# The softmax sums of twelve batches: three accumulating transfers over tap planes instead of VectorE reductions

## The chip, the cores and the metric

One Trainium2 chip, of which the kernel uses one core. A core has five engines that run side by side, each taking its own instructions strictly in order: TensorE (PE, matrix products into PSUM), VectorE (DVE, elementwise work and reductions), ScalarE (ACT, functions such as exponential and ReLU, and copies out of PSUM), GpSimd (POOL) and SyncE (SP). POOL and SP mainly issue transfers (DMAs), which the core's 16 DMA engines carry out. An engine that meets an instruction whose input is not there yet waits, and everything behind that instruction on the same engine waits with it. The metric is device time in microseconds (us) of one execution; the median of several runs is given.

## What is computed

A dynamic convolution followed by a layer with two hidden products. For each of 8 sequences of 4160 positions and 8 heads, a softmax over 7 taps gives weights, with which the last 7 positions of `x` are summed; each head owns 24 of 192 channels. The result, 33280 rows of 192, goes through two products with 1024 hidden columns, of which the larger is kept, and through a product back to 192 columns.

```python
w = np.exp(weight_gen - max over taps)
w = w / (np.sum(w, axis=-1, keepdims=True) + 1e-09)
out[b, s, h, :] = sum over k of w[b, s, h, k] * x_pad[b, s + k, h, :]      # h: 24 channels
g = np.maximum(out @ w1, out @ w2)                                         # 192 -> 1024
return g @ w_out                                                           # 1024 -> 192
```

The kernel takes no maximum off. It forms the weight as exp(w - ln(sum of exp(w))), so that a softmax costs one exponential, a sum over 7 taps, a logarithm, a subtraction and a second exponential.

## The kernel before

**Tiling.** The 33280 rows lie as 128 partitions x 260 columns, a column being one row for each partition. Columns go in 17 batches (`BATCHES`): 0 to 15 of 16 columns, and one last of 4. A batch of index 2 to 15 is worked in two units of 8 columns, batches 0 and 1 in four units of 4. TensorE's work is counted in 260 tiles: a unit of 8 columns has 8 tiles, each one chunk of 128 hidden columns for all 8 columns of the unit. Tiles go in groups, two at a time for the first 16, three at a time later (`GROUPS`).

**One batch's way through the engines.**

1. `load_wg` (L104): weights of a batch, 128 x 896 (16 columns x 8 heads x 7 taps) from HBM into `wg_t`, issued on POOL.
2. `exp_sum` (L135, ScalarE): exponential of `wg_t` into `e_t`. The taps of one column and head lie side by side, 7 elements.
3. `red` (L147, VectorE): the sum of 7 neighbours, 128 x 448 to 128 x 64, twice per batch, into `sum_t`.
4. `ln` (L151, ScalarE): logarithm of the 128 x 128 sums in place.
5. `shift` (L156, VectorE): subtracts it from `wg_t`, in three parts.
6. `weights` (L167, ScalarE): second exponential, into `en_t` in bf16, each weight twice, read from `wg_t` with a step of 7 elements.
7. `mul` (L182, VectorE): 7 taps x 8 columns of `x` times the weights into `m_t`, 128 x 10752 in bf16; then `adds` (L198, L204, L207, VectorE): the 7 taps are summed pairwise into `y_t`.
8. `transpose` (L216, SP): `y_t` is transposed by a transfer into `yt`. On POOL, `gate` (L224), a copy of one column of `yt`, holds the loads behind it until that transpose has landed: for a unit at column 0, `xb_t` for 8 columns (L114) and `wg_t` of three batches later (L104); for a unit at column 8, `xb_t` for the next batch and its halo, a copy of 6 columns within SBUF (`load_halo`, L127).
9. `hid_tile` (L299, TensorE) makes the hidden products from `yt`, `relu` (L309, ScalarE) takes them out of PSUM into `rd_t`, `out_first` and `out_second` (L351, L339, TensorE) make the output products, `evac` (L395, ScalarE) copies them to `o_t`, and SP stores them (L407).

**What sets the order.** The order of every engine is the order in which the program is written. TensorE's groups are the frame. ScalarE's softmax steps for batches from 3 on stand in a table, `due`, by the index of a tile, and are written out with the group that holds that tile (`softmax_steps`). A long step (exponentials) is put off by a group where a long one has just stood in a group with few outputs. The rows for batch c:

```python
ln_at = -2 if c == 4 else 0 if c < 8 else 2 if c < 11 else 4
parts_.append((16 * (c - 2) + ln_at, False, lambda c=c: ln(c)))
parts_.append((16 * (c - 3) + (4 if c < 8 else 7), True, lambda c=c: exp_sum(c)))
```

VectorE's steps stand in `extra(t)`, which is called for each tile. The two halves of `red` are written beside the adds of an earlier batch, and the three parts of `shift` beside others:

```python
adds(c, 0, beside=lambda i, of: shift(c + 1, i, of) if c + 1 < NB else None)
...
adds(b + 1, 8, beside=lambda i, of: red(b + 3, i, 2) if b + 3 < NB and i < 2 else None)
```

`e_t` has two buffers, `sum_t` three, `wg_t` four and `yt` six.

Of the kernel before, what the change touches and what calls it, by code (L numbers as in the profile page):

```python
# [9 lines left out]
FP32 = mybir.dt.float32  # L10
BF16 = mybir.dt.bfloat16
I32 = mybir.dt.int32
AF = mybir.ActivationFunctionType
ALU = mybir.AluOpType
# [3 lines left out]
def _sub(base: bass.AP, off: int, dims):  # L18
    ap = [list(base.ap[0])] + [[int(s), int(c)] for s, c in dims]
    return dataclasses.replace(base, offset=base.offset + off, ap=ap)  # L20
# [3 lines left out]
def kernel(  # L24
# [9 lines left out]
    nc = tc.nc  # L34

    B, S, D = x.shape
    H, K = weight_gen.shape[2], weight_gen.shape[3]
    F = moe_w1.shape[1]
    P = 128
# [10 lines left out]
    BATCHES = [(c, min(16, CPP - c)) for c in range(0, CPP, 16)]  # L50
    NB = len(BATCHES)


    def pieces(b):
        n = BATCHES[b][1]
        at, done = [], 0
        for w in (4, 4, 4, 4) if b < 2 else (8, 8) if n == 16 else (n,):
            at.append((done, w))
            done += w
        return at  # L60
# [18 lines left out]
    psm = ctx.enter_context(tc.tile_pool(name="psm", bufs=3))  # L79
# [17 lines left out]
    wg_ts, xb_ts, e_ts, s_ts, en_ts, y_ts, yt_ts = {}, {}, {}, {}, {}, {}, {}  # L97
# [33 lines left out]
    def exp_sum(b, i=0, of=1):  # L131
        if i == 0:
            e_ts[b] = pe_.tile([P, BATCHES[b][1] * WGC], FP32, name="e_t", tag="e")
        w = BATCHES[b][1] * WGC // of
        nc.scalar.activation(out=e_ts[b][:, i * w:(i + 1) * w], in_=wg_ts[b][:, i * w:(i + 1) * w], func=AF.Exp)  # L135

    def part(b, i, of):

        n = BATCHES[b][1]
        h0, h1 = n * i // of * H, n * (i + 1) // of * H  # L140
        return slice(h0, h1), h0 * K, [[K, h1 - h0], [1, K]]

    def red(b, i=0, of=1):
        if i == 0:
            s_ts[b] = psm.tile([P, BATCHES[b][1] * H], FP32, name="sum_t", tag="sum")
        hs, at, ap = part(b, i, of)
        nc.vector.reduce_sum(out=s_ts[b][:, hs], in_=_sub(e_ts[b], at, ap), axis=AX.X)  # L147

    def ln(b, i=0, of=1):
        s_t = s_ts[b][:, part(b, i, of)[0]]  # L150
        nc.scalar.activation(out=s_t, in_=s_t, func=AF.Ln)  # L151

# [6 lines left out]
    def weights(b, o):  # L159

        w = dict(pieces(b))[o]
        if b not in en_ts:
            en_ts[b] = pen.tile([P, 16 * WGC * 2], BF16, name="en_t", tag="en")
        J = 2 if w == 4 and b < 2 else 1
        N = w * H // J
        for j in range(J):
            nc.scalar.activation(  # L167
                out=_sub(en_ts[b], (o * WGC + j * N * K) * 2, [[2 * N, K], [2, N], [1, 2]]),
                in_=_sub(wg_ts[b], (o * H + j * N) * K, [[1, K], [K, N], [0, 2]]), func=AF.Exp,
            )  # L170
# [62 lines left out]
    def half(j):  # L233
        return slice(64 * j, 64 * j + 64)
# [191 lines left out]
    OUTS, c = [[], [], []], 0  # L426
# [85 lines left out]
    with tc.tile_pool(name="pstage", bufs=1) as pstage:  # L512
# [7 lines left out]
        for p0, p1 in ((1, 16), (16, P)):  # L520
            nc.sync.dma_start(  # L521
                out=xs[p0:p1, 0:PAD * D],
                in_=bass.AP(tensor=x.tensor, offset=(p0 * CPP - PAD) * D,
                            ap=[[CPP * D, p1 - p0], [1, PAD * D]]),
# [20 lines left out]
        for wi, wsrc in enumerate((moe_w1, moe_w2)):  # L545
            for h in range(2):
                nc.sync.dma_start(
                    out=ws["T", wi][half(h), :],
                    in_=bass.AP(tensor=wsrc.tensor, offset=P * F + h * HF, ap=[[F, 64], [1, HF]]),
# [11 lines left out]
        for step in (exp_sum, red, ln, shift):  # L561
            for i in range(2):
                step(0, i, 2)
# [6 lines left out]
        for o in (0, 4, 8, 12):  # L570
            weights(0, o)
        nc.vector.tensor_copy(out=xb_ts[0][:, PAD * D:(PAD + 4) * D],
                              in_=xs[:, PAD * D:(PAD + 4) * D])
# [36 lines left out]
        def keep_warm(times):  # L610
# [11 lines left out]
            out=wo[:, :].rearrange("p (f d) -> p f d", d=D),  # L622
            in_=bass.AP(tensor=moe_w_out.tensor, offset=0, ap=[[D, P], [P * D, FCH], [1, D]]),
# [11 lines left out]
        hid_tile(0)  # L635
        relu(rd, 0, 1)
        exp_sum(1)
        hid_tile(1)
        relu(rd, 1, 1)
        w_diff(1, nc.vector.tensor_copy)  # L640
        sum_transpose(1)
        red(1)
        mul(0, 8)
        hidden(1)
        ln(1)
        shift(1)
        mul(0, 12)
# [39 lines left out]
        mul(1, 4)  # L687
        relu(rd, 7, 1)
        exp_sum(2)
        red(2)  # L690
        adds(1, 4, True)
        sum_transpose(3)
# [9 lines left out]
    def end_of_1():  # L702
# [12 lines left out]
                     behind(yt_of[4], load_wg(4, nc.gpsimd))), end_of_1),  # L715
        5: (lambda: sum_transpose(5, LEFT), none),
        6: (lambda: (behind(relu_of[12], load_x(2, 8, 8)), weights(2, 8), ln(3), sum_transpose(6, LEFT)), none),
        7: (lambda: (behind(relu_of[14], load_x(3, 0, 8)), sum_transpose(7, LEFT)), none),
    }

    due = {}
    for c in range(3, NB):
        soon = c < 8
        parts_ = [(16 * (c - 2) + (8 if soon else 10 if c < NB - 1 else 15), True, lambda c=c: weights(c, 0))]
        if 8 in dict(pieces(c)):
            parts_.append((16 * (c - 2) + (14 if soon else 15), True, lambda c=c: weights(c, 8)))
        if c > 3:
            ln_at = -2 if c == 4 else 0 if c < 8 else 2 if c < 11 else 4
            parts_.append((16 * (c - 2) + ln_at, False, lambda c=c: ln(c)))
            parts_.append((16 * (c - 3) + (4 if c < 8 else 7), True, lambda c=c: exp_sum(c)))  # L730
        for t, *step in parts_:
            due.setdefault(t, []).append(step)
    waiting, long_in_two = [], [False]
# [86 lines left out]
```

## Time and profile before

| | |
|---|---|
| median of 3 runs (410.8, 415.66, 410.81) | 410.81 us |
| span of the profiled execution, first to last instruction | 409.1 us |
| exponential of 128 x 896, L135, mean | 0.977 us |
| logarithm of 128 x 128, L151, mean | 0.336 us |
| halo copy within SBUF, L127, time on POOL | 0.547 us |
| `gate`, L224, mean | 1.171 us |
| DMA bytes moved | 65.68 MB, mean 161 GB/s |
| granted TensorE clock | full, but for the last slice and rounding |

The profile is one execution. "Busy" is the time in which an engine works on an instruction; matmuls overlap, so TensorE's busy time is not a measure of how near it is to its peak. The chain of waits is followed back from the last instruction: at each step to what released it, or, where it waited for nothing, to the instruction before it on its engine. The slices of the span, 40 in all, give busy tenths by engine:

```
PE   7999999999999999999999999999999999999995
DVE  6999999999999999999999999999999999999000
ACT  6899989999999988999988999988999989888771
POOL 0321101222211021221101221210122212210000
DMA  8966667658657874963796497489648648744513
```

### The profile page before, as it was taken

To read this page: it belongs to the slowest core of one execution; us is meant where nothing else is said; L and a number is where in the kernel's file an instruction comes from. 1 tells how busy PE (TensorE), PEld (TensorE's weight loads), DVE (VectorE), ACT (ScalarE), POOL (GpSimd) and SP (SyncE) were. 2 spreads that over 40 slices of the span, in tenths; PEclk is the share of its full clock that TensorE was granted. 3 is DMA by queue.
4 is the path that set the end of the run, shared out by engine and by line. 5 is a ranking of instruction groups with operands and counts; after the bars stand their busy time and mean duration, and the time that the engine had idled before them with its cause. 6 is when DMAs were issued, how large, how long until landed. Compare 5 with 4: busy or idle time off the path is not lost.

```text
span 409.1 us, 15992 instructions
## 1 busy us (share of the span) xinstructions
PE 398.8 (97%) x7350; PEld 317.1 (78%) x7350; DVE 374.4 (92%) x219; ACT 357.4 (87%) x424; POOL 68.7 (17%) x101
## 2 busy tenths in 40 slices
PE   7999999999999999999999999999999999999995
PEld 2688999677777777777777777777787777787795
DVE  6999999999999999999999999999999999999000
ACT  6899989999999988999988999988999989888771
POOL 0321101222211021221101221210122212210000
PEclk9999999999999999999999999999999999999998
DMA  8966667658657874963796497489648648744513
GB/s 245 250 152 164 116 151 186 143 143 184 150 97 219 217 118 99 260 176 74 224 195 146 96 251 180 82 195 238 120 106 241 166 64 244 151 89 79 213 61 136
DMA packets 60384, 65.68 MB, mean 161 GB/s; under 512 B 47615, under 2 KB 48511, under 8 KB 60318
## 3 DMA queue, kind: packets, MB, share of 16 engines
q1 hardware_dynamic: 51934, 40.54, 36.0%
q0 software_dynamic: 8240, 24.04, 29.5%
q8 instruction: 57, 0.93, 0.9%
q10 hardware_dynamic: 144, 0.10, 0.1%
q14 instruction: 9, 0.07, 0.1%
HBM read 35.96 MB, written 25.56 MB: 150 GB/s over the span
## 4 chain that ended last, share of the span: by engine, by line
DVE 73%; PE 17%; issue 4%; DMA 4%; SPq 0%; DVEq 0%; ACT 0%
DVE m_t L182 37%; DVE m_t L198 15%; DVE m_t L204 10%; PE op_ps L339 9%; PE hd L299 7%; DVE sum_t L147 3%; DVE y_t L207 3%; DVE wg_t L156 3%; DMA xs<-in_x_dram 3%; PE op_ps L351 2%; DMA yt<-y_t 1%; DVE wd L582 0%; DVE xb_t L618 0%; SPq L521 0%; SPq L104 0%
## 5 line engine op out<-in xcount | busy, mean ns | idle before, releaser
L309 ACT ACTIVATE rd_t<-hd 128x1024 bf16<-128x1024 f32 (+1 forms) x206 | 234.6, 1189 | 28.0 <-PE hd L299 26.5
L339 PE MATMUL op_ps<-wo,rd_t 64*128 64x192 bf16 x4160 | 210.6, 243 | 0.1
L339 PEld LDWEIGHTS <-rd_t 64*128 64x128 bf16 x4160 | 180.8, 94 | 15.7 <-ACTq L372 0.3
L299 PE MATMUL hd<-yt,wd 64*128 64x512 bf16 (+1 forms) x1584 | 187.3, 360 | 1.4 <-ACT rd_t L309 1.2
L182 DVE TENSOR_TENSOR m_t<-xb_t,en_t 128x10752 bf16<-128x10752 bf16 (+1 forms) x37 | 187.4, 5071 | 0.2
L299 PEld LDWEIGHTS <-wd 64*128 64x128 bf16 x1776 | 94.1, 94 | 43.3 <-issue 3.3
L224 POOL CAST gate<-yt 128x1 f32<-128x1 bf16 x29 | 34.0, 1171 | 275.7 <-DMA yt<-y_t 275.7
L198 DVE TENSOR_TENSOR m_t<-m_t 128x4608 bf16<-128x4608 bf16 (+1 forms) x32 | 76.8, 2401 | 0.1
L395 ACT COPY o_t<-op_ps 128x384 f32<-128x384 f32 (+1 forms) x99 | 57.3, 591 | 13.4 <-PE op_ps L339 13.3
L351 PE MATMUL op_ps<-w,yt 64*128 64x192 bf16 x780 | 55.5, 243 | 1.1 <-ACT o_t L395 1.0
L351 PEld LDWEIGHTS <-yt 64*128 64x128 bf16 x780 | 38.4, 94 | 17.5 <-issue 2.1
L204 DVE TENSOR_TENSOR m_t<-m_t 128x3072 bf16<-128x3072 bf16 (+1 forms) x29 | 50.0, 1724 | 0.1
L167 ACT ACTIVATE en_t<-wg_t 128x896 bf16<-128x896 f32 (+2 forms) x45 | 35.3, 820 | 0.0
L207 DVE TENSOR_TENSOR y_t<-m_t 128x1536 bf16<-128x1536 bf16 (+1 forms) x29 | 27.3, 941 | 0.5
L385 DVE COPY o_last<-op_ps 128x192 f32<-128x192 f32 x1 | 0.4, 358 | 25.9 <-ACT o_last L385 25.9
L156 DVE TENSOR_TENSOR wg_t<-wg_t,sum_t 128x280 f32<-128x280 f32 (+5 forms) x46 | 22.0, 481 | 0.0
L147 DVE TENSOR_REDUCE sum_t<-e_t 128x64 f32<-128x448 f32 (+2 forms) x31 | 19.6, 636 | 2.6 <-ACT e_t L135 2.6
L114 POOL DMA_DIRECT2D xb_t<-in_x_dram x33 | 17.7, 535 | 23.3 <-ACT rd_t L309 11.8
L135 ACT ACTIVATE e_t<-wg_t 128x896 f32<-128x896 f32 (+2 forms) x18 | 16.1, 899 | 2.5 <-DMA wg_t<-in_weight_gen_dram 2.5
L309 ACT ACTIVATE rd_t<-hdp 128x1024 bf16<-128x1024 f32 x16 | 16.2, 1048 | 0.6 <-PE hdp L299 0.6
L613 PE MATMUL warm<-ident 128*128 128x512 bf16 x38 | 11.0, 457 | 2.6 <-DVE ident L560 2.6
L299 PE MATMUL hdp<-yt,wd 64*128 64x256 bf16 x192 | 12.9, 269 | 0.1
(46 smaller groups left out, 73.6 us busy)
## 6 DMA issues: line engine op xcount, KB each, us to landing
out_dram<-o_t SPq DMA_DIRECT2D x28, 768.0 KB, 5.0
xb_t<-in_x_dram POOLq DMA_DIRECT2D x30, 384.0 KB, 5.2
wg_t<-in_weight_gen_dram POOLq DMA_DIRECT2D x14, 448.0 KB, 5.2
xb_t<-xb_t POOLq DMA_DIRECT2D x16, 288.0 KB, 5.2
out_dram<-o_t SPq DMA_DIRECT2D x8, 384.0 KB, 2.9
wg_t<-in_weight_gen_dram SPq DMA_DIRECT2D x2, 448.0 KB, 4.5
xs<-in_x_dram SPq DMA_DIRECT2D x2, 384.0 KB, 6.0
xb_t<-in_x_dram POOLq DMA_DIRECT2D x3, 192.0 KB, 5.1
```

The source lines that it names most:

```text
L156: nc.vector.tensor_tensor(out=w_t, in0=w_t, in1=_sub(s_ts[b], hs.start, [[1, hs.stop - hs.start], [0, K]]), op=ALU.subtract)
L167: nc.scalar.activation(out=_sub(en_ts[b], (o * WGC + j * N * K) * 2, [[2 * N, K], [2, N], [1, 2]]), in_=_sub(wg_ts[b], (o * H + j * N) * K ...
L182: return nc.vector.tensor_tensor(out=m_out, in0=x_in, in1=_sub(en_ts[b], o * WGC * 2, [[2, K * n * H], [0, G // 2], [1, 2]]), op=ALU.mult,)
L198: nc.vector.tensor_tensor(out=taps(0, 1, 3), in0=taps(0, 1, 3), in1=taps(3, 1, 3), op=ALU.add)
L204: nc.vector.tensor_tensor(out=taps(0, 2, 2), in0=taps(0, 2, 2), in1=taps(1, 5, 2), op=ALU.add)
L207: nc.vector.tensor_tensor(out=_sub(y_ts[b], o * D, [[64, 2], [P, 3 * w // 2], [1, 64]]), in0=taps(0, 1, 1), in1=taps(2, 1, 1), op=ALU.add,)
L224: nc.gpsimd.tensor_copy(out=gate, in_=yt[:, 0:1])
L299: nc.tensor.matmul(hid_out(t, f, j), lhsT=wd_at(j, s, f // 4, f % 4 * P, P), rhs=_sub(yt_ts[u][half(j), :], (s + j) % 3 * P, [[3 * P, w // ...
L309: relu_of[t0] = nc.scalar.activation(out=rd[:, k * 1024:(k + n) * 1024], in_=hd[:, at:at + n * 1024], func=AF.Relu)
L339: return nc.tensor.matmul(op_out(c), lhsT=rd[half(r), k * 1024 + at:k * 1024 + at + P], rhs=wo[half(r), f * D:(f + 1) * D], start=False, s ...
L351: nc.tensor.matmul(op_out(c + j), lhsT=yt_ts[u][half(j), (3 * i + (s + j) % 3) * P:(3 * i + (s + j) % 3 + 1) * P], rhs=w10[half(j), s * D: ...
L395: nc.scalar.copy(out=_sub(o, c % 24 * D, [[D, len(qs)], [h * D, 2], [1, D]]), in_=_sub(tile_, at + (qs[0] - p) * D, [[D, len(qs)], [512, 2 ...
```

## The change

For batches 4 to 15 (`by_dma`) the exponential writes `e_t` as 7 planes of 128 sums' terms, one for each tap, instead of with the 7 taps side by side; it reads `wg_t` with a step of 7. Right behind it, three transfers on POOL's queue add planes onto planes within `e_t`, each of them reading what the one before wrote: planes 0 to 2 += planes 3 to 5, planes 0 and 1 += planes 2 and 6, plane 0 += plane 1. `red` does nothing for these batches. The logarithm reads plane 0 of `e_t` and writes `sum_t`. The exponential's due tile moves from 4 to 2 (batches 4 to 7) and from 7 to 5 (8 to 15) within its batch's table. Batches 0 to 3 and 16 are as before.

```diff
     def exp_sum(b, i=0, of=1):
         if i == 0:
             e_ts[b] = pe_.tile([P, BATCHES[b][1] * WGC], FP32, name="e_t", tag="e")
+        if by_dma(b):
+            N = BATCHES[b][1] * H
+            nc.scalar.activation(out=_sub(e_ts[b], 0, [[N, K], [1, N]]), in_=_sub(wg_ts[b], 0, [[1, K], [K, N]]),
+                                 func=AF.Exp)
+            return
...
+    def by_dma(b):
+        return 4 <= b < NB - 1
+
+    def tap_planes(b):
+        N, e_t = BATCHES[b][1] * H, e_ts[b]
+        for to, frm in (((0, [[1, 3 * N]]), (3 * N, [[1, 3 * N]])),
+                        ((0, [[N, 2], [1, N]]), (2 * N, [[4 * N, 2], [1, N]])),
+                        ((0, [[1, N]]), (N, [[1, N]]))):
+            nc.gpsimd.dma_start(out=_sub(e_t, *to), in_=_sub(e_t, *frm), accum_op=ALU.add)
...
     def red(b, i=0, of=1):
+        if by_dma(b):
+            return
...
     def ln(b, i=0, of=1):
+        if by_dma(b):
+            N = BATCHES[b][1] * H
+            s_ts[b] = psm.tile([P, N], FP32, name="sum_t", tag="sum")
+            nc.scalar.activation(out=s_ts[b], in_=e_ts[b][:, 0:N], func=AF.Ln)
+            return
...
-            parts_.append((16 * (c - 3) + (4 if c < 8 else 7), True, lambda c=c: exp_sum(c)))
+            at = 2 if by_dma(c) and c < 8 else 4 if c < 8 else 5 if by_dma(c) else 7
+            parts_.append((16 * (c - 3) + at, True,
+                           lambda c=c: (exp_sum(c), by_dma(c) and tap_planes(c))))
```

On POOL the three transfers of a batch stand behind the halo copy of the unit at column 8 and ahead of the next `gate`. Each carries 128 partitions x 384, 2 x 128 and 128 elements of fp32.

## The prediction

> **What bounds the kernel now.** I read the page first (engines, slices, chain), then the waits, the PE, POOL and ACT rows in order of time, then durations by shape and times to landing.
>
> ```profile
> PE 398.8 (97%) x7350; PEld 317.1 (78%) x7350; DVE 374.4 (92%) x219; ACT 357.4 (87%) x424; POOL 68.7 (17%) x101
> ...
> DVE 73%; PE 17%; issue 4%; DMA 4%; SPq 0%; DVEq 0%; ACT 0%
> ```
>
> The chain gives VectorE 73% of the span, and the edit takes work from VectorE. But the chain steps onto VectorE at one single place, a wait of 0.2 us:
>
> ```profile
> ACT rd_t L309 <- PE hd L299: 26.5, 53, 0.8
> ...
> PE hd L299 <- ACT rd_t L309: 1.2, 5, 0.3
> ...
> PE hd L299 <- DMA yt<-y_t: 0.2, 1, 0.2
> ```
>
> The last row is all that TensorE waits for VectorE's results (`y_t`, transposed into `yt`) in the whole run. The reader is to see that a chain's share is not a bound. In order of time:
>
> ```profile
> 204.97 1.48 PE L299 MATMUL hd<-yt,wd 64*128 64x512 bf16 x12
> ...
> 213.61 1.47 PE L299 MATMUL hd<-yt,wd 64*128 64x512 bf16 x12
> ```
>
> Six tiles in 8.64 us, 1.44 us a tile; the same 8.64 us returns in nearly every such stretch from 63 us to the end, with the granted clock at 1.00. Eight columns therefore cost TensorE 11.52 us. VectorE needs 11.82 us for the same eight (its L207 starts at 208.79 and 220.61), so it is slightly slower and lives off a lead from the start: the transpose landed at 61.7 us for matmuls at 68.9, at 203.1 for 205.6, and at 333.45 for 333.50. The lead is used up just when the work ends. TensorE is the bound; VectorE is about to be one.
>
> **The change, part by part.**
>
> *Removed from VectorE.* 24 reductions:
>
> ```profile
> L147 DVE TENSOR_REDUCE sum_t<-e_t 128x64 f32<-128x448 f32 x26 | 15.9, 614 | 2.6 <-ACT e_t L135 2.6
> L135 ACT ACTIVATE e_t<-wg_t 128x896 f32<-128x896 f32 x15 | 14.6, 977 | 0.0
> L167 ACT ACTIVATE en_t<-wg_t 128x896 bf16<-128x896 f32 x28 | 29.4, 1063 | 0.0
> ```
>
> 24 x 0.614 = 14.7 us of VectorE's 374.4, 1.2 us in each 23.6 us batch. On the path this is worth the 0.2 us above and, at most, the stretches longer than 8.64 us (8.97, 8.77, 8.91, 8.79, 9.02: 1.3 us in excess together, part of it ScalarE's). Nor can VectorE run far ahead: its next need is the shift L156, which waits for the logarithm L151, and that stands in ScalarE's order among the ReLUs of TensorE's tiles. At 262 us the logarithm ends at 261.8 and the shift starts at 262.7, so 0.9 us of lead can be won there. I count the gain at 0.
>
> *ScalarE.* The exponential now reads with a step of 7 elements and writes 7 planes. L167 reads with that step and takes 1.06 us against 0.98: 12 x 0.09 = 1.0 us more, at nothing on the path, because ScalarE idles 26.5 us waiting for `hd`, and stretches with an exponential already last 8.64 us. The far bound is the 128x2048 ReLU of L309, 1.90 us, 0.92 us more than now. The stretch with two `en_t` and a logarithm (182.30 to 191.26, about 1 us more ScalarE work than those with one) is 0.33 us longer, so the high end is 12 x 0.33 = 4 us. I take 0, the row with the same step. The order moves little, since tiles come in threes: only the exponentials of batches 4, 10 and 13 go forward, by 3, 2 and 2 tiles, and two `en_t` near tile 28 by 4. The logarithm keeps its place.
>
> [...]
>
> *Added: a chain of three transfers, each waiting on POOL for the one before.* Exponential end to logarithm start is the time it has. From the L135 and L151 rows, with the three moves applied, and with POOL's own halo before it for 13: batch 4 14.4 us, 5 16.1, 6 14.3, 7 and 8 17.2, 9 11.3, 10 19.1, 11 19.0, 12 16.3, 13 17.7, 14 19.0, 15 16.3. Batch 9 is the tight one: its exponential ends at 175.7, its logarithm starts at 187.0. The logarithm heads ScalarE's queue; behind it stand the ReLUs that empty PSUM for TensorE, so lateness there is TensorE's, less what the pipeline absorbs (one `en_t` plus logarithm, 1.4 us, costs nothing, 2.4 us costs 0.33: some 0.65 us is free; for batch 9, which is in that longer stretch, none).
>
> No accumulating transfer is in the trace. The nearest row is the copy within SBUF on the same queue:
>
> ```profile
> xb_t<-in_x_dram POOLq DMA_DIRECT2D x30, 384.0 KB, 5.2
> wg_t<-in_weight_gen_dram POOLq DMA_DIRECT2D x14, 448.0 KB, 5.2
> xb_t<-xb_t POOLq DMA_DIRECT2D x16, 288.0 KB, 5.2
> ```
>
> Issue to landing is 5.2 us in the median, but behind an `xb_t` load in the queue. The one that had little ahead of it (30.06 us) landed in 2.55; the slowest took 6.95. The new transfers carry 192, 128 and 64 KB of result, less than 288, and follow no load; but they add, which no row prices, and share the engines with transposes and stores (`xb_t` loads of one size take from 4.5 to 6.8 us). Bounds: 3 x 2.55 = 7.7 and 3 x 6.95 = 20.9 us. I take 4.0 each, about midway between the lone copy and the median: 12 us, plus 0.1 us a wake-up, 12.3. Only batch 9 is late, by 1.0 us.
>
> [...]
>
> *What queues behind it on POOL.* The third transfer is issued two landings after the first, and then come the gate L224 and two loads:
>
> ```profile
> 178.16 1.78 POOL L224 CAST gate<-yt 128x1 f32<-128x1 bf16 x1 [9.02 <-DMA yt<-y_t]
> 179.88 0.53 POOL L114 DMA_DIRECT2D xb_t<-in_x_dram  x1
> 180.40 0.55 POOL L104 DMA_DIRECT2D wg_t<-in_weight_gen_dram  x1
> ```
>
> At 4.0 us for batch 9: 175.7 + 8.2 + 0.55 = 184.5, gate 1.2, `xb_t` issued at 185.7 instead of 179.9 and landed 5.5 us later, at 191.2; its multiply starts at 197.8. Covered. `wg_t` lands 2h + 7.55 us after an exponential that a load waits behind (h for one transfer): 15.6 us at h = 4. The closest next exponentials are batch 10's, 16.2 us later, and batch 13's, 16.6 us: covered by 0.6 us, and a ScalarE stall from h = 4.3 on. SP's queue gets no new wait; transfers add about 0.4 MB a batch to 3.8 MB.
>
> *Sum.* Span 409.1 + 1.0 = 410.1 us. The runs' median, 410.81, lies 1.7 above that span; 411.8 us.
>
> **Rivals.** (a) *Slower: the chain is late for the logarithm in many batches.* For it: a median of 5.2 on the nearest row, and adding is extra. Against: that row's load in front. At h = 5.6 the chain takes 17.1 us: late by 2.7, 1.0, 2.8, 5.8, 0.8 and 0.8 (batches 4, 5, 6, 9, 12, 15), and `wg_t` by 2.55 and 2.15 (10, 13): 18.6 us, less 7 x 0.65, is 14; 423 + 1.7 = 425 us. It decides from h = 5.2, where the same sum gives 8.2 us, 2%. At h = 6 it gives 23.7 us, 434; at the slowest row's 6.95, 460 and more.
> (b) *Faster: VectorE set the pace after all,* as the chain of waits suggests, and all 14.7 us come off: 396 us. Against: the 0.2 us and the even 8.64 us. A real gain of 2% would need TensorE under 1.41 us a tile, and it shows 1.44 in stretches where nothing is late.
> (c) *The strided exponential stalls ScalarE:* 4 us more, 416 us, still within 2% of 410.81.
>
> **How the numbers follow.** A run of this kernel can be told from no change at about 2%, 8.2 us. My forecast with (c) has 0.54, its own range 409.5 to 418; (a) has 0.43, because the one quantity that decides is on no row and its edge, 5.2 us, is the nearest row's median; (b) 0.03. These are also the chances of within, slower and faster. The range goes from 409.5 to 434, where (a) has reached h = 6: nearly all of the first case and about two thirds of the second.
>
> **What would show it.** Right: VectorE busy near 360 us, with new idle before L156 (its line moves down) released by the logarithm; the three `e_t<-e_t` landings near 4 us each; ScalarE idle before a logarithm only in batch 9, about 1 us; six tiles still 8.64 us. Wrong on transfers: a large row of ScalarE's logarithm waiting for a DMA into `e_t`, and TensorE's `hd` waiting for `rd_t`. Wrong on the stride: exponentials well over 1.1 us. Wrong on the bound: six tiles clearly under 8.64 us. And if `wg_t` is late, the exponential of batches 10 and 13 waits for its load.

## The result, and the profile after

| | before | after |
|---|---|---|
| median | 411.36 us (4 runs, 410.8 to 415.66) | 426.53 us (4 runs, 425.1 to 431.08) |
| ratio to before, 95% interval | | 1.0362 [1.0279, 1.0446] |
| profiled execution, span | 409.1 us | 429.3 us (its run: 431.08) |

The change makes the kernel 3.6% slower. The time lies in the forecast's range (409.5 to 434) and close to rival (a)'s 425, and 14.7 us above the forecast's 411.8; the ratio is known to about 0.8% either way. The profiled execution is the longest of the four. Where the median and the ratio of a kernel below do not go together (e4, e6, e7, e11), the ratio leaves out one or two runs that took over 1.5% longer than the kernel's fastest.

In the changed kernel the lines have moved: exponential into planes L136 (ordinary L140), transfers L152, reductions L166, logarithm of plane 0 L172, `shift` L180, multiply L206, `gate` L248, hidden products L323, ReLU L333, output products L363 and L375, `evac` L419; loads and halo are still L104, L114, L127. First the engines and the chain of waits, then two groups and the times to landing, all from the page of after:

```profile
PE 402.3 (94%) x7350; PEld 318.8 (74%) x7350; DVE 365.1 (85%) x195; ACT 367.3 (86%) x424; POOL 125.9 (29%) x137
...
PE 59%; ACT 16%; DMA 13%; issue 7%; POOL 4%; SPq 1%; DVE 0%; POOLq 0%; ACTq 0%; DVEq 0%
...
L152 POOL DMA_DIRECT2D e_t<-e_t x36 | 36.0, 1000 | 140.4 <-DMA e_t<-e_t 80.4
...
L136 ACT ACTIVATE e_t<-wg_t 128x896 f32<-128x896 f32 x12 | 22.6, 1882 | 5.9 <-DMA wg_t<-in_weight_gen_dram 5.9
...
xb_t<-in_x_dram POOLq DMA_DIRECT2D x30, 384.0 KB, 6.5
wg_t<-in_weight_gen_dram POOLq DMA_DIRECT2D x14, 448.0 KB, 6.7
...
e_t<-e_t POOLq DMA_DIRECT2D x12, 192.0 KB, 4.2
e_t<-e_t POOLq DMA_DIRECT2D x12, 128.0 KB, 4.0
```

VectorE did lose its work and has left the chain: 73% before, 0% now. It is busy for 365.1 us instead of 374.4; that is 9.3 us less and not 14.7, because its instructions overlap a little in the record, by 15.6 us in all before and 10.5 now. TensorE, DMA and POOL stand in its place. A transfer lands 4 us after its issue, as forecast. POOL stands still for 80.4 us waiting for the landings of its own transfers, as two landings of 4 us in each of twelve batches had it. Two things were not forecast: the exponential takes 1.88 us instead of 0.98; and the loads, issued behind those waits, land later (medians of 5.2 us before, 6.5 and 6.7 now).

The waits of after, in total us, times, longest us:

```profile
POOL e_t L152 <- DMA e_t<-e_t: 80.4, 23, 5.9
...
POOL xb_t L127 <- DMA xb_t<-in_x_dram: 41.9, 12, 5.5
...
DVE wg_t L180 <- ACT sum_t L172: 24.2, 10, 3.8
...
ACT sum_t L172 <- DMA e_t<-e_t: 6.0, 2, 3.4
ACT e_t L136 <- DMA wg_t<-in_weight_gen_dram: 5.9, 3, 5.4
ACT e_t L140 <- DMA wg_t<-in_weight_gen_dram: 5.3, 2, 2.7
...
PE hd L323 <- ACT rd_t L333: 4.6, 5, 1.2
```

The second row is POOL's halo copy waiting for late `xb_t` loads (5.4 us before). The third is VectorE's relief: it arrives at `shift` early and waits there for ScalarE. The fourth and fifth are ScalarE's new waits for transfers, few and long; of the sixth, one wait stood in before too (2.5 us), the other, 2.6 us, is that of batch 16's exponential. Where they fell shows in time order. The table gives the time of six tiles, from the start of the first hidden product of the tile named to that of the tile six on; where nothing is late it is 8.64, and less in the first stretches. It shows all stretches that differ by over 0.4 us, with those of four experiments told of below.

| from tile | before | after | e2 | e3 | e8 | e9 |
|---|---|---|---|---|---|---|
| 16 | 7.11 | 8.46 | 8.46 | 8.45 | 8.47 | 8.46 |
| 52 | 7.52 | 8.36 | 8.36 | 8.37 | 8.37 | 8.38 |
| 88 | 8.64 | 9.09 | 8.69 | 9.25 | 8.66 | 8.68 |
| 112 | 8.97 | 12.88 | 8.96 | 8.97 | 8.97 | 8.97 |
| 118 | 8.64 | 9.06 | 8.59 | 13.59 | 8.59 | 8.59 |
| 166 | 8.64 | 17.65 | 8.67 | 17.27 | 8.67 | 8.69 |
| 172 | 8.64 | 8.64 | 8.64 | 8.64 | 11.35 | 8.64 |
| 214 | 9.02 | 10.24 | 8.59 | 9.91 | 8.59 | 8.59 |

Of the 20.2 us between the two spans, 9.0 are lost at tile 166 and 3.9 at 112; 3.1 were already lost before tile 16, where no changed instruction has run (that start lies between 47.4 and 51.0 us in the profiles of the kernels here, e1's the latest). The rest is 1.35, 0.38 (tile 34) and 0.84 us in the first stretches, 1.2 at 214 (batch 16's late load), and 0.4 each at 88 and 118. POOL around the large stop, in time order (start, duration, what, and in brackets the idle time before and what ended it):

```profile
256.60 0.87 POOL L152 DMA_DIRECT2D e_t<-e_t  x1 [3.74 <-ACT e_t L136]
265.86 1.23 POOL L152 DMA_DIRECT2D e_t<-e_t  x1 [8.39 <-issue]
271.75 0.91 POOL L152 DMA_DIRECT2D e_t<-e_t  x1 [4.67 <-DMA e_t<-e_t]
272.33 0.53 POOL L248 CAST gate<-yt 128x1 f32<-128x1 bf16 x1
272.45 0.90 POOL L114 DMA_DIRECT2D xb_t<-in_x_dram  x1
273.00 0.93 POOL L104 DMA_DIRECT2D wg_t<-in_weight_gen_dram  x1
273.55 0.56 POOL L248 CAST gate<-yt 128x1 f32<-128x1 bf16 x1
273.67 0.90 POOL L114 DMA_DIRECT2D xb_t<-in_x_dram  x1
```

and ScalarE in the same stretch:

```profile
275.19 0.31 ACT L172 ACTIVATE sum_t<-e_t 128x128 f32<-128x128 f32 x1 [3.36 <-DMA e_t<-e_t]
280.90 1.85 ACT L136 ACTIVATE e_t<-wg_t 128x896 f32<-128x896 f32 x1 [5.40 <-DMA wg_t<-in_weight_gen_dram]
```

These are batch 12's three transfers. They land 8.17, 5.61 and 3.36 us after their issues, the last at 275.12 (the second is issued 1.1 us after the first has landed, which the view puts down to issue), and the logarithm has waited 3.36 us for it. The load of `wg_t` for batch 13 could not be issued until the third transfer was; it goes out at 273.00, in a bunch with two `xb_t` loads (two gates run together, since both units' `yt` are there by then, landed at 261.12 and 271.82), lands 7.88 us later, and the exponential of batch 13, next long step in ScalarE's order, waits 5.40 us more. ScalarE's ReLUs stand behind both, and TensorE stops for 6.3 us.

### The profile page after: what moved, and what is told of

Same layout as the page of the kernel before. It is cut to its first block, busy times and chain, and to the rows that moved or that the text cites. A ratio compares the mean times of both kernels' runs of the same rounds, so it can differ in the third digit from the quotient of the medians.

```text
span 429.3 us, 15997 instructions
## 1 busy us (share of the span) xinstructions
PE 402.3 (94%) x7350; PEld 318.8 (74%) x7350; DVE 365.1 (85%) x195; ACT 367.3 (86%) x424; POOL 125.9 (29%) x137
## 4 chain that ended last, share of the span: by engine, by line
PE 59%; ACT 16%; DMA 13%; issue 7%; POOL 4%; SPq 1%; DVE 0%; POOLq 0%; ACTq 0%; DVEq 0%
PE op_ps L363 26%; PE hd L323 25%; ACT rd_t L333 9%; DMA e_t<-e_t 6%; PE op_ps L375 5%; DMA wg_t<-in_weight_gen_dram 5%; ACT e_t L136 3%; POOL gate L248 2%; POOL e_t L152 2%; DMA ws1T<-in_moe_w_dram 2%; ACT o_t L419 1%; PE hdp L323 1%; PE yps L272 1%; ACT yt L279 1%; ACT en_t L191 1%
## 5 line engine op out<-in xcount | busy, mean ns | idle before, releaser
L333 ACT ACTIVATE rd_t<-hd 128x1024 bf16<-128x1024 f32 (+1 forms) x206 | 233.5, 1188 | 23.5 <-PE hd L323 22.9
L363 PE MATMUL op_ps<-wo,rd_t 64*128 64x192 bf16 x4160 | 212.7, 244 | 6.4 <-ACTq L396 6.3
L363 PEld LDWEIGHTS <-rd_t 64*128 64x128 bf16 x4160 | 182.4, 95 | 22.8 <-ACTq L396 7.1
L323 PE MATMUL hd<-yt,wd 64*128 64x512 bf16 (+1 forms) x1584 | 188.4, 361 | 4.6 <-ACT rd_t L333 4.6
L206 DVE TENSOR_TENSOR m_t<-xb_t,en_t 128x10752 bf16<-128x10752 bf16 (+1 forms) x37 | 187.5, 5071 | 0.6 <-ACT en_t L191 0.4
L323 PEld LDWEIGHTS <-wd 64*128 64x128 bf16 x1776 | 94.7, 94 | 47.5 <-issue 8.3
L152 POOL DMA_DIRECT2D e_t<-e_t x36 | 36.0, 1000 | 140.4 <-DMA e_t<-e_t 80.4
L248 POOL CAST gate<-yt 128x1 f32<-128x1 bf16 x29 | 60.0, 2068 | 54.9 <-DMA yt<-y_t 54.9
L419 ACT COPY o_t<-op_ps 128x384 f32<-128x384 f32 (+1 forms) x99 | 57.3, 592 | 12.1 <-PE op_ps L363 12.1
L375 PE MATMUL op_ps<-w,yt 64*128 64x192 bf16 x780 | 55.6, 243 | 5.2 <-ACT o_t L419 5.0
L375 PEld LDWEIGHTS <-yt 64*128 64x128 bf16 x780 | 38.4, 94 | 22.5 <-issue 8.2
L180 DVE TENSOR_TENSOR wg_t<-wg_t,sum_t 128x280 f32<-128x280 f32 (+5 forms) x46 | 22.1, 483 | 24.4 <-ACT sum_t L172 24.2
L114 POOL DMA_DIRECT2D xb_t<-in_x_dram x33 | 27.1, 821 | 25.0 <-DVE m_t L206 10.8
L136 ACT ACTIVATE e_t<-wg_t 128x896 f32<-128x896 f32 x12 | 22.6, 1882 | 5.9 <-DMA wg_t<-in_weight_gen_dram 5.9
L127 POOL DMA_DIRECT2D xb_t<-xb_t x16 | 8.8, 548 | 41.9 <-DMA xb_t<-in_x_dram 41.9
L104 POOL DMA_DIRECT2D wg_t<-in_weight_gen_dram x15 | 14.6, 973 | 12.0 <-ACT rd_t L333 5.0
L333 ACT ACTIVATE rd_t<-hdp 128x1024 bf16<-128x1024 f32 x16 | 16.3, 1046 | 1.2 <-PE hdp L323 1.1
```

The lines of the kernel that those rows point to most:

```text
L136: nc.scalar.activation(out=_sub(e_ts[b], 0, [[N, K], [1, N]]), in_=_sub(wg_ts[b], 0, [[1, K], [K, N]]), func=AF.Exp)
L152: nc.gpsimd.dma_start(out=_sub(e_t, *to), in_=_sub(e_t, *frm), accum_op=ALU.add)
L206: return nc.vector.tensor_tensor(out=m_out, in0=x_in, in1=_sub(en_ts[b], o * WGC * 2, [[2, K * n * H], [0, G // 2], [1, 2]]), op=ALU.mult,)
L248: nc.gpsimd.tensor_copy(out=gate, in_=yt[:, 0:1])
L323: nc.tensor.matmul(hid_out(t, f, j), lhsT=wd_at(j, s, f // 4, f % 4 * P, P), rhs=_sub(yt_ts[u][half(j), :], (s + j) % 3 * P, [[3 * P, w // ...
L333: relu_of[t0] = nc.scalar.activation(out=rd[:, k * 1024:(k + n) * 1024], in_=hd[:, at:at + n * 1024], func=AF.Relu)
```

## The experiments

Theory A: TensorE sets the pace and the transfers as such cost nothing; the loss is POOL's queue standing still for two landings per batch, which makes the logarithm and then the load of `wg_t` late. Rivals: the slower exponential; the transfers' traffic or their adds; the logarithm's wait alone.

**e1 and e2: without the transfers.** In e1 the reductions are dropped and nothing takes their place; in e2 the exponential writes planes, at its moved place.

```diff
 # e1, of the kernel after
-            nc.scalar.activation(out=_sub(e_ts[b], 0, [[N, K], [1, N]]), in_=_sub(wg_ts[b], 0, [[1, K], [K, N]]), ...
+            nc.scalar.activation(out=e_ts[b], in_=wg_ts[b], func=AF.Exp)
...
-            at = 2 if by_dma(c) and c < 8 else 4 if c < 8 else 5 if by_dma(c) else 7
+            at = 4 if c < 8 else 7
 # e1 and e2
-                           lambda c=c: (exp_sum(c), by_dma(c) and tap_planes(c))))
+                           lambda c=c: exp_sum(c)))
```

> The kernel before without the 24 reductions of batches 4 to 15 and without anything in their place; the logarithm takes the first 128 elements of e_t, so the softmax sums of these batches are left out. It prices the removal alone. Theory A (TensorE is the bound, the time was lost in a few places where ScalarE waits): 409 to 411.5 us, ratio 0.995 to 1.002, six tiles still 8.64 us, VectorE near 360 us busy. Rival (VectorE set the pace): 14.7 us less, about 396 us, ratio 0.965.

> The changed kernel without the three transfers; the logarithm reads plane 0 as the exponential wrote it, so the sums over taps of batches 4 to 15 are left out. It keeps the exponential into planes (1.88 us) and its earlier place. Theory A: the slower exponential alone costs ScalarE 11 us and the end almost nothing, 410 to 414 us, ratio 1.00 to 1.01, six tiles 8.6 to 8.7 us. Rival B (the loss is spread: the slower exponential delays the ReLUs in every batch): 418 us or more.

e1: 410.75 us, 0.9968 [0.9938, 0.9999]. e2: 413.35 us, 1.0040 [1.0010, 1.0070]. Sums that cost nothing at all are worth 0.3%: 14.7 us of VectorE's work were not on the path, and with ScalarE's steps in this order no form of this change could have gained much more than that (0.6% by the interval's end). The slower exponential costs 2.6 us, the difference of the two medians, and the first stretches account for it: from tiles 16, 34 and 52 (batches 4 to 6) six tiles take 1.35, 0.38 and 0.84 us longer than before, together 2.57, and those of the later batches no longer. In e2 batch 4's exponential also stands three tiles earlier than in e1, and no run parts that from its length; those of 5 and 6 stand where they stood. The 2.6 us explain a sixth of the loss of 15.2 us.

**e3: the logarithm does not wait.** It reads plane 4, which no transfer writes.

```diff
-            nc.scalar.activation(out=s_ts[b], in_=e_ts[b][:, 0:N], func=AF.Ln)
+            nc.scalar.activation(out=s_ts[b], in_=e_ts[b][:, 4 * N:5 * N], func=AF.Ln)
```

> The changed kernel with its three transfers as they are, but the logarithm reads plane 4, which no transfer writes, so that it does not wait for them (the sums over taps of batches 4 to 15 are left out of the result). POOL's queue, its loads and the DMA traffic are as in the change. Theory A has two kinds of stop: the logarithm's of batch 9 and 12 (2.6 and 3.4 us of ScalarE waiting) go, the exponential's wait for the late wg_t in batches 13 and 16 (5.4 and 2.6 us) stays at 3 to 8 us in sum: 414 to 420 us. If the logarithm's wait was all: 411 us. If traffic on the DMA engines or POOL was it: 424 us or more.

428.24 us, 1.0407 [1.0346, 1.0469]: no gain at all, where 414 to 420 was expected. The waits of e3:

```profile
ACT e_t L136 <- DMA wg_t<-in_weight_gen_dram: 10.5, 3, 6.2
```

The logarithm's row is gone, and the load's has grown from 5.9 to 10.5 us. The stop at tile 112 went (8.97 us), and one at 118 came (13.59), where the exponential of batch 10 waits for its load. Both waits lie behind the same queue, one behind the other, and taking one away uncovers the other. The rival "the logarithm alone" falls.

**e4: batches 9 and 12 go back to VectorE.**

```diff
-        return 4 <= b < NB - 1
+        return 4 <= b < NB - 1 and b not in (9, 12)
```

> The change for ten of its twelve batches: 9 and 12, the two whose logarithm or whose successor's exponential comes soonest, keep the reductions of VectorE. Theory A: the two large stops (stretches of 12.9 and 17.7 us instead of 8.64) go, 411 to 415 us, ratio 1.00 to 1.01. Rival B (a cost of each batch with transfers): ten twelfths of the 15 us stay, 423 to 425 us.

419.78 us, 1.0163 [1.0076, 1.0249], between theory A's 411 to 415 and rival B's 423 to 425. The stops at 112 and 166 are gone (8.97 and 8.82 us), but 154 and 178 take 9.29 and 9.50, and 214 still 10.17. About half of the loss is cured by two batches of twelve; the interval is too wide to say how much more than half.

**e5: reading in order, writing with a step.** The exponential reads `wg_t` as it lies and writes the planes with a step of 128 elements.

```diff
-            nc.scalar.activation(out=_sub(e_ts[b], 0, [[N, K], [1, N]]), in_=_sub(wg_ts[b], 0, [[1, K], [K, N]]), ...
+            nc.scalar.activation(out=_sub(e_ts[b], 0, [[1, N], [N, K]]), in_=_sub(wg_ts[b], 0, [[K, N], [1, K]]), ...
```

> The change, with the exponential walking wg_t in order and writing the planes with a step of 128 elements, in place of reading with a step of 7 and writing in order; the result is the same. If the strided read costs: the exponential takes 0.95 to 1.1 us again instead of 1.88, each chain starts 0.8 us sooner, stops shrink by 1 to 2 us each, 421 to 425 us. If the strided write costs as much: 1.9 us and 426 us as before.

426.61 us, 1.0359 [1.0294, 1.0424]; its exponential takes 1.83 us, against 1.88 in after and 0.98 in order. The step is dear on either side, and the time did not move. As a test of what a shorter exponential brings, it failed: it did not make it shorter.

**e6, e7, e8: the load of `wg_t` one gate earlier.** e6 does that alone, e7 with e5's edit, e8 with e3's, so that in e8 neither the logarithm nor the exponential waits.

```diff
-        if o == 0 and b + 3 < NB:
+        if u == 8:
             load_wg(b + 3, nc.gpsimd)
+        if o == 8 and b + 4 < NB:
+            load_wg(b + 4, nc.gpsimd)
```

> The change, with each wg_t load issued one gate earlier on POOL (at the unit at column 8, ahead of the three transfers, instead of behind them). Theory A now: two waits share the loss, the load of wg_t behind the transfers (batches 10, 13, 16) and the late logarithm (9, 12). Earlier loads take the first away: the exponentials of 10, 13 and 16 wait for nothing, the logarithms of 9 and 12 still wait 2 to 4 us each; 416 to 420 us. If the loads were all: 411 to 413 us. If the late logarithm makes up for it (one wait in place of the other): 424 us or more.

> Both: earlier wg_t loads and the exponential that reads in order. Theory A: what is left is the late logarithm of batches 9 and 12, shortened by 0.8 us each; 414 to 418 us. If the exponential's write with a step is no cheaper, as with earlier loads alone.

> The change with earlier wg_t loads, and with the logarithm reading plane 4, which no transfer writes (the sums over taps of batches 4 to 15 are left out of the result). Neither ScalarE's logarithm nor its exponential waits for anything on POOL. Theory A (these two waits are all of the loss): 411 to 414 us, close to the kernel without transfers (413.35), six tiles 8.6 to 8.8 us throughout. If POOL's late xb_t loads or the DMA engines' load cost as well: 418 us or more.

e6: ratio 1.0176 [1.0089, 1.0264]; e7: 1.0279 [1.0199, 1.0359]; e8: 418.37 us, 1.0139 [1.0103, 1.0175]. e6's four runs take 417.2 to 425.4 us, against 425.1 to 431.1 for after: it is faster by the ratio, but how much stays open. e7, whose exponential is as long as e5's, stayed above the 416 to 420 that were expected for that case. In its profile no exponential of a plane batch waits for its load any more, but the logarithm still waits, 5.2 us in two places. With both waits gone, e8 keeps a loss of 1.4%, of which e2's exponential is 0.4. That is its rival's "418 us or more" and not theory A's 411 to 414: the two waits are not all of the loss. Of the 4.7 us between the profiles of e8 and e2, 1.7 lie before tile 16 and 2.7 in the stretch from tile 172, where there is a third wait, in the waits of e8:

```profile
PE hd L325 <- DMA yt<-y_t: 2.5, 1, 2.5
```

At 273.11 SP issues a transpose. POOL, held until then by the halo's wait for its load, issues three transfers just before it:

```profile
271.99 0.54 POOL L127 DMA_DIRECT2D xb_t<-xb_t  x1 [4.29 <-DMA xb_t<-in_x_dram]
272.52 0.55 POOL L104 DMA_DIRECT2D wg_t<-in_weight_gen_dram  x1
273.06 0.93 POOL L152 DMA_DIRECT2D e_t<-e_t  x1
```

SP adds two stores at 274.6 and 276.8. The 16 DMA engines' mean busy share, which the view lets go above 1, is 0.91, 1.26 and 0.85 in the three slices of 4 us from 273 us; the transpose lands after 9.4 us (median 3.9 in before), the accumulating transfer after 9.2. TensorE waits 2.5 us for `yt`, and the stretch from tile 172 takes 11.35 us. That the crowding makes the transpose late is read from this trace; no run tests it alone.

**e9 and e11: the waiting or the transfers?** e9 keeps three accumulating transfers of the same sizes behind each exponential, but into a tile of their own (`aside`), so that none waits for another (the planes read and written are set to match, in lines not shown); the logarithm reads plane 4. e11 keeps the chain and its waits but copies instead of adding.

```diff
 # e9
-            nc.gpsimd.dma_start(out=_sub(e_t, *to), in_=_sub(e_t, *frm), accum_op=ALU.add)
+            nc.gpsimd.dma_start(out=_sub(aside, *to), in_=_sub(e_t, *frm), accum_op=ALU.add)
 # e11
-            nc.gpsimd.dma_start(out=_sub(e_t, *to), in_=_sub(e_t, *frm), accum_op=ALU.add)
+            nc.gpsimd.dma_start(out=_sub(e_t, *to), in_=_sub(e_t, *frm))
```

> Three accumulating transfers of the same sizes at the same place on POOL, but none waits for another: each adds planes of e_t onto a tile of its own, and the logarithm reads plane 4, which nothing writes (the sums over taps of batches 4 to 15 are left out of the result). Same bytes, same number of transfers as in the change. Theory A (the loss is POOL standing still for two landings, about 8 us a batch, and what then comes late or in a bunch): 411 to 415 us, close to the kernel without transfers (413.35), no stretch over 9.3 us. Rival D (the added transfers themselves crowd the DMA engines, or accumulating disturbs the transposes): 418 us or more, with slow transposes.

> The change with plain copies in place of the three accumulating transfers, same sizes, places and waits (the sums over taps of batches 4 to 15 are left out of the result). It prices the adding. If the add costs a second read of about 1 us: issue to landing 3.0 to 3.3 us instead of 4, 417 to 422 us. If adding is free: 4 us each and 425 us or more as in the change.

e9: 413.25 us, 1.0039 [1.0024, 1.0054], the same as e2 without any transfer (1.0040). From its waits:

```profile
POOL aside L152 <- ACT e_t L136: 77.5, 12, 10.6
```

and the times to landing of its page:

```profile
wg_t<-in_weight_gen_dram POOLq DMA_DIRECT2D x14, 448.0 KB, 6.3
...
aside<-e_t POOLq DMA_DIRECT2D x12, 192.0 KB, 4.0
aside<-e_t POOLq DMA_DIRECT2D x12, 128.0 KB, 4.6
```

The transfers land about as late as in after (4.0 and 4.6 us against 4.2 and 4.0), and `wg_t` takes 6.3 us against 6.7. Bytes, adds and number of transfers are the same. POOL waits for exponentials, but never for the landing of one of the three, the loads go out in time, and nothing is lost: the rival of traffic and adds falls. What e9 leaves out is the chain: both the standing queue and the logarithm's dependence on it. e3's logarithm does not depend on the transfers either: between its 1.0407 and e9's 1.0039 only POOL's waits for landings differ, and the tile that is written. So the standing queue is the cause.

e11: 1.0110 [1.0054, 1.0166], median 415.77, less than either of the expected 417 to 422 and 425. POOL still waits 91.3 us for landings. The whole chain takes 11.4 us in the mean against 13.1 (its hops have medians of 3.9, 3.2 and 2.3 us, against 4.2, 4.0 and 3.5), and some 10 us of the loss are gone; of ScalarE's waits for transfers in plane batches, 1.3 us for `wg_t` are left. Two things follow. By these medians an add costs 0.3 to 1.2 us a transfer, and what that time consists of no run shows; but with the same adding transfers the medians of e3 and e5 lie up to 0.7 us from those of after, so that the figure is rough. And the waiting of POOL is not itself the price: the price is what comes late by it, and it sets in steeply, since e5's chains, 12.3 us in the mean, still cost 3.6%, and e11's of 11.4 cost 1%.

**e10 and e12: the chain without the standing queue.** Batches 6 to 15; the second and third transfer are issued behind the next two gates, where the one before has landed, and `wg_t` is loaded a gate earlier. In e10 the exponential is due 8 tiles earlier than in after (5 for batches 6 and 7); in e12 it is due 16 earlier than in the kernel before (19 for batch 8), and `wg_t` is loaded one gate earlier still.

```diff
-        for to, frm in (((0, [[1, 3 * N]]), (3 * N, [[1, 3 * N]])),
...
+        leg((0, [[1, 3 * N]]), (3 * N, [[1, 3 * N]]))
+        legs.append(lambda: leg((0, [[N, 2], [1, N]]), (2 * N, [[4 * N, 2], [1, N]])))
+        legs.append(lambda: leg((0, [[1, N]]), (N, [[1, N]])))
...
+        if o == 8 and b + 4 < NB:        # e12: o == 0
+            load_wg(b + 4, nc.gpsimd)
+        if legs:
+            legs.pop(0)()
...
-            at = 2 if by_dma(c) and c < 8 else 4 if c < 8 else 5 if by_dma(c) else 7
+            at = -3 if by_dma(c) else 4 if c < 8 else 7     # e12: (-12 if c < 9 else -9) if by_dma(c)
```

> The change's sums for batches 6 to 15, spread out: the first transfer behind the exponential, the second and third each behind the next two gates, so that POOL finds the landing before it done; exponentials 8 tiles earlier and wg_t loads one gate earlier, to make room. Theory A: POOL waits for e_t landings nearly nothing, 411 to 415 us, no better than before since TensorE is the bound. If a late logarithm shows again (the third transfer lands 1 to 3 tiles before it): up to 420 us. Rival D (the transfers' traffic): 418 us or more without such waits.

> What is changed against the run with the second and third transfer behind the next two gates: the exponentials of batches 6 to 15 stand a whole batch of tiles earlier than in the kernel before (tile 4 or 7 of the batch's table, as there), so that they no longer share six tiles with a second exponential (`en_t`), and `wg_t` is loaded half a batch earlier for that, behind the gate of the unit at column 0. Nothing is left out; batches 4 and 5 keep VectorE's sums. That run took 418.4 us, with seven stretches of six tiles of 9.6 to 10.1 us, all of them holding an exponential and an `en_t`, and no engine waiting for a transfer. Theory A (those 8 us are ScalarE's crowding; with POOL's queue no longer standing still the transfers themselves cost nothing): no stretch much over 9 us, 411 to 414 us, within 1% of before. Rival B (those stretches are long because of the transfers, which now lie beside the transposes and loads of every unit): long stretches remain, at other places, with TensorE's `hd` waiting for `yt` or `rd_t`, 416 us or more. In neither theory is it faster than before by 1%: TensorE's 1.44 us a tile stays.

e10: 418.37 us, 1.0165 [1.0136, 1.0194]; e12: 415.24 us, 1.0081 [1.0053, 1.0109]. POOL waits 2.2 and 3.0 us for landings of `e_t`, and neither kernel has a logarithm or a plane exponential waiting for a transfer. e10 still lost more than e9, and more than theory A's 411 to 415: seven stretches of 9.6 to 10.1 us cost it some 8 us, and ScalarE in one of them (tile 160) shows why:

```profile
258.84 1.90 ACT L136 ACTIVATE e_t<-wg_t 128x896 f32<-128x896 f32 x1
260.60 1.06 ACT L196 ACTIVATE en_t<-wg_t 128x896 bf16<-128x896 f32 x1
```

Two long steps now stand side by side, and ScalarE is busy for 9.60 of the stretch's 9.60 us: here the 1.88 us does cost. e12 takes them apart, and the seven stretches are gone (those from 112, 130, 160 and 178 take 8.91, 8.64, 8.73 and 8.59). Left are 9.74 us at tile 34, where the exponentials of batches 5 and 6 meet and ScalarE is busy all the time, and 9.19 at 118 and 166, where it is busy for 8.54 and 8.88; those two stay unexplained. The time lies between A's 414 and B's 416, the ratio within A's 1%, its interval up to 1.1%; the cure of the seven stretches speaks for A. No version with the transfers beats the kernel before, and e1 leaves none of this kind more than its 0.3%, or 0.6% at its interval's end.

## Why the prediction was right, and where it was wrong

The time lies in the range, but in the part that was added for rival (a): the forecast's own part, 409.5 to 418 with a chance of 0.54, did not hold, and the change is not "no change" but slower.

**The bound: right.** TensorE sets the pace, stretches with nothing late still take 8.64 us, and the 14.7 us of VectorE are worth 0.3% (e1). The wait of 0.2 us told more than the chain's 73%; rival (b) is out.

**The exponential: wrong.** "I take 0, the row with the same step" was the choice, at 1.06 us. It measured 1.88, near the far bound of 1.90. The row L167 reads each element twice and writes bf16, so it was not the row of this access. e2 repeats the length, 1.89 us, and e5 shows nearly the same price on the write side, 1.83; why such a step costs that much no run shows. The term was 0 to 4 us, taken as 0, and it measured 2.6, nearer to rival (c); but (c) spread it over twelve batches at 0.33 us, and it fell on the first three alone.

**The landing time: right in the median, wrong as a sum.** h = 4.0 was taken, and 4.2, 4.0 and 3.5 measured. The mean chain was 13.1 us against 12.3, batch 9's 12.7. The 0.1 us a wake-up in those 12.3 was an estimate: in batch 9 the logarithm started 0.1 us after the last landing, but POOL issued the next transfer some 0.3 us after a landing. But twelve chains were summed as twelve medians. Batch 12's hops took 8.17, 5.61 and 3.36, and the first of them fell where the DMA engines' share was 0.95 to 1.33. By windows of after (the column before the last is their mean busy share, which goes above 1 here):

```profile
253.00:257.00 4.00, 4.00 (x74) 3.15 (x71) 4.00 (x4) 4.00 (x5) 0.40 (x1) 1.00 0.95 169
257.00:261.00 4.00, 4.00 (x74) 3.11 (x70) 3.97 (x2) 3.71 (x5) 0.47 (x1) 1.00 1.33 164
```

A load, a halo, a transpose and a store were in flight beside it. Batch 9 was said to be late by 1.0 us; it was late by 2.6: 0.9 from the longer exponential, 0.4 from the chain, the rest not resolved.

**The load behind the chain: the step that failed.** "`wg_t` lands 2h + 7.55 us after an exponential that a load waits behind ...: covered by 0.6 us, and a ScalarE stall from h = 4.3 on." Mechanism, place and batch were right: the exponential of 13 waited for its load. The size was not. The 15.6 us measured 24.6 (exponential of 12 over at 256.30, load landed at 280.88): 6.3 from the two hops, wake-ups and longer issues, and 2.7 from the load itself, 7.88 us where 5.2 was taken. A margin of 0.6 us was counted as cover against terms whose own spread in the trace of before, 4.5 to 6.8 us for `xb_t` loads of one size, was four times as wide; `wg_t`'s own loads took up to 8.8 us there. And the two latenesses of batch 12, logarithm and load, add on ScalarE (3.36 + 5.40 us); the forecast had neither, and rival (a)'s sum had them as 0.8 and 2.15 us.

**Rival (a): right on the sign, near in size by luck, and not in its condition.** It had its 425 us from h = 5.6 in every batch, and decided from 5.2. The medians stayed at 4, and most of the price came behind two batches in twelve: behind 12 by hops of 8.17 and 5.61 us and by the load, behind 9 by a chain of 12.7 us. Of its 18.6 us the late logarithms were 13.9 and the late loads 4.7; the logarithms are not the decisive part, since e3 without their wait is no faster.

## What to carry to other kernels

A wait for a landing that stood in the issuing queue delayed every load behind it and then let them out in a bunch: behind batch 12's third transfer three loads went out within 1.2 us, the one for `wg_t` landing after 7.88 us (median 5.2 in before). Price such a wait by the slowest landings in the trace and by the tightest load behind it, not by medians: a margin smaller than the spread of its own terms is no cover. When one late result is cured and the time does not move, look in the same queue for the next one before dropping the theory. And before relieving the busiest engine, ask what the bound engine ever waited for it: 0.2 us here, against 73% of a chain.

## What the runs showed of the hardware

**Stride.** An exponential of 128 x 896 in fp32 takes 0.98 us in order, 1.88 reading with a step of 28 bytes, 1.83 writing with a step of 512 bytes. With the same reading step but each element read twice in a row, and bf16 written, 128 x 896 outputs take 1.06.

**Issue.** POOL's issue takes 0.88, 1.22 and 0.90 us for the three accumulating transfers, and 0.61 in the mean for plain copies of the same shapes (e11).

**A stop costs more than itself.** TensorE around the stop at 275 us, in time order, and then by windows (the last three columns are the granted clock, the DMA share and GB/s):

```profile
280.98 2.74 PE L363 MATMUL op_ps<-wo,rd_t 64*128 64x192 bf16 x32 [6.31 <-ACTq L396]
```

```profile
281.00:284.00 3.00, 2.72 (x32) 2.34 (x33) 3.00 (x2) 3.00 (x2) 0.88 (x1) 0.50 0.59 164
284.00:290.00 6.00, 5.30 (x76) 3.56 (x77) 5.96 (x2) 6.00 (x8) 1.22 (x1) 1.00 1.05 330
```

Thirty-two such matmuls take 1.50 us where nothing is late (as at 205.34 us): the clock was at half for the 3 us behind the stop, which adds 1.24 us to the 6.3. After the gap of 2.92 us at batch 9 it was 0.61 in the mean from 198 to 201 us, and half from 198.65 to 202.05.
